# Summing softmax-free attention denominators without TensorE: seven of eight units by copies between partition groups

## The chip, the cores and the metric

The kernel runs on one core of a Trainium2 chip. The core has a matrix engine (TensorE, PE in the profile), a vector engine (VectorE, DVE), an engine for pointwise functions (ScalarE, ACT), a general engine (GpSimd, POOL) and one that issues transfers (SyncE, SP). On-chip memory (SBUF) has 128 partitions, and so has PSUM, in which TensorE puts its results, in banks of 512 fp32 columns. The metric is the device time of one execution, in microseconds (us).

## The reference

Two independent blocks of linear attention, A and B, whose outputs are put side by side. S is 2048 tokens, D is 640, and there are 32 heads of 20.

```python
qkv = (x @ wqkv).reshape(B, S, 3, H, Dh)            # q, k, v by head
phi = lambda t: where(t > 0, t + 1, exp(t)) + 1e-6
pq, pk = phi(q), phi(k)
kv  = einsum("bhsd,bhse->bhde", pk, v)
z   = einsum("bhsd->bhd", pk)
num = einsum("bhqd,bhde->bhqe", pq, kv)
den = einsum("bhqd,bhd->bhq", pq, z)[..., None] + 1e-6
out = (num / den) @ wo
```

The denominator is one number for each token and head: the sum of that head's 20 features of pq, each weighted by z.

## The kernel before

Matrices are multiplied in a 32-bit form of reduced precision. A factor is split into a high part, rounded by a ScalarE copy, and a low part, the difference, made by VectorE; a product is the sum of three matmuls, high by high, high by low and low by high. The first half of the kernel works on keys and values under a planner and is untouched. It ends at about 290 us. For each block it leaves z, and a matrix M (values and the output weights folded together), so that the output of a token is its pq, divided by its denominators, times M.

The second half goes over eight units of 512 tokens, four of block A (0 to 3) and four of block B (4 to 7). Its order is written out by hand: the loop at the end of the function calls, for each unit u, five query steps and then the output of unit u - 1. A query step (`qmm`, lines 924 to 926) is 15 matmuls of 512 columns for one of five groups of 128 features, followed by `qphi`, exp and relu on ScalarE (L1092, L1093) and their join on VectorE (L1094), and `qacc`, which adds the features weighted by z into an accumulator of 128 partitions by 512 tokens (L1102 on ScalarE for the first group, L1104 on VectorE for the others).

Features lie so that partition p holds head p mod 32. So after five groups the accumulator holds four partial sums for each head, in partitions 0 to 31, 32 to 63, 64 to 95 and 96 to 127. To add these four and have the sum in all four places at once, the kernel multiplies by the constant matrix `same`, which has a 1 where two partitions agree mod 32. This is the chain of the denominators: `split_acc` (high part on ScalarE at L918, low part on VectorE at L915), `denmm` (two matmuls into PSUM, L1114 and L1115), `recip` (a reciprocal on VectorE for each half of 256 tokens, L1120) and `divide` (L1126), which scales all of pq. Then `d_sums` (L1142 to L1147), `a_split` and `d_split` prepare the stationary factors of the output product, called da and ds, with h for high and l for low parts.

The output (`outmm`, L1203) is one level of a seven-product recursion for two 256-token halves q: 14 steps of six or nine matmuls of 320 columns. Its partial sums are the PSUM tiles pa, pe and psb. ScalarE copies pa into the output tile o (L1218), VectorE adds psb and pe (L1219). A later step goes on accumulating in the same pa, so it waits for the copy of the step before.

What stands between these is hung into slots: ("q", u, c, k) lies behind the three matmuls k of query step c of unit u, and ("o", u, s) behind output step s of unit u. The table `chain` gives the slots of the denominators' chain. Unit 0's chain runs during the queries of unit 1, that of unit v from 1 to 6 during the output of unit v - 1, and what it leaves is used in the output of v. `split` only issues ScalarE's copy; the VectorE part is kept in a list and issued at the next slot. Each engine does its own instructions in order.

Other work hangs in the same slots: the roundings of the raw queries (L962, tile xqh), of wo (tile woh, low part wol), copies of M out of PSUM (L1008, tile mev) and the forms of M for the recursion (tile fsh).

Of the kernel before, what the change touches and what calls it, by code (L numbers as in the profile page):

```python
# [7 lines left out]
F32 = mybir.dt.float32  # L8
# [3 lines left out]
AF = mybir.ActivationFunctionType  # L12
OP = mybir.AluOpType
# [205 lines left out]
def tile_linear_attn_pair(ctx: ExitStack, tc: tile.TileContext, ins, out: bass.AP):  # L219
    nc = tc.nc  # L220
    P = 128
# [19 lines left out]
    kx, kg, q1a, q1b, q2, q3 = [], [], [], [], [], []  # L241
# [435 lines left out]
    a, z, x = jh[0][0:P], jl[0][0:P], jr[0][0:P]  # L677
# [117 lines left out]
    for p in range(4, NPB):  # L795
        i, h = divmod(p - 2, 2)
# [9 lines left out]
    for p in range(NPB + 1, NP):  # L806
        if p == NPB + 1:
            fl = kvs
        else:
            i, h = divmod(p - NPB - 2, 2)  # L810
# [70 lines left out]
    for g, (h0, nh) in enumerate(GROUPS):  # L881
        cols = NC * DH * nh
        w = Space("wv", cols, (BD,))
# [17 lines left out]
    def bank(name, tag="one", bufs=3):  # L901
        at, n = ptags[tag]
        pn[tag] = pn.get(tag, -1) + 1
        return psum.tile([P, 512], F32, name=name, tag=f"bank{at + pn[tag] % n}", bufs=1)
# [165 lines left out]
    pq, acc, den, dd = {}, {}, {}, {}  # L1070
# [39 lines left out]

    def denmm(u):
        t = acc.pop(u)
        ps = den.pop(u) if u in den else bank("psd", "small", 1)
        nc.tensor.matmul(ps, same, t[:, 0], start=True, stop=False)  # L1114
        nc.tensor.matmul(ps, same, t[:, 1], start=False, stop=True)  # L1115
        den[u] = (ps, q2[0].tile([P, 512], F32, name="rd", tag="rd", bufs=1))

    def recip(u, h):
        ps, r = den[u]
        nc.vector.reciprocal(r[:, h * 256:(h + 1) * 256], ps[:, h * 256:(h + 1) * 256])  # L1120

    def divide(u, h):

        r = den[u][1][:, h * 256:(h + 1) * 256].unsqueeze(1).to_broadcast([P, NC, 256])
        p = pq[u][:, :, h * 256:(h + 1) * 256]
        nc.vector.scalar_tensor_tensor(p, p, EPS, r, op0=OP.add, op1=OP.mult)  # L1126

    da, ds, sr = {}, {}, {}
# [161 lines left out]
    h = NG - 1  # L1290
# [8 lines left out]
    for c in range(NC):  # L1299
# [3 lines left out]
        for u in range(1, NU - 1):  # L1303
# [3 lines left out]

    at(("q", 1, 0, 0), z_end)

    den[0] = bank("psd", "small", 1)  # L1310

    chain = {
        0: [(("q", 1, 0, 0), split_acc, 0), (("q", 1, 1, 1), denmm, 0), (("q", 1, 1, 1), recip, 0, 0),
            (("q", 1, 1, 1), recip, 0, 1), (("q", 1, 1, 2), divide, 0, 0), (("q", 1, 1, 4), divide, 0, 1),
            (("q", 1, 2, 0), d_sums, 0, 0), (("q", 1, 2, 2), a_split, 0, 0), (("q", 1, 2, 4), d_sums, 0, 1),
            (("q", 1, 3, 1), d_split, 0, 0), (("q", 1, 3, 4), a_split, 0, 1), (("q", 1, 4, 1), d_split, 0, 1)]}
    for v in range(1, NU):
        w, u = v - 1, v + 1
        if v == NU - 1:
            chain[v] = [(("o", w, 1), split_acc, v), (("o", w, 4), denmm, v), (("o", w, 4), recip, v, 0),  # L1320
                        (("o", w, 5), divide, v, 0), (("o", w, 6), a_split, v, 0, 0), (("o", w, 6), d_sums, v, 0, 0),
                        (("o", w, 7), d_split, v, 0, 0), (("o", w, 8), a_split, v, 1, 0), (("o", w, 8), d_sums, v, 1, 0),
                        (("o", w, 9), recip, v, 1), (("o", w, 10), d_split, v, 1, 0), (("o", w, 12), divide, v, 1),
                        (("o", v, 0), a_split, v, 0, 1), (("o", w, 13), d_sums, v, 0, 1),
                        (("o", v, 0), d_split, v, 0, 1), (("o", v, 2), d_sums, v, 1, 1),
                        (("o", v, 2), a_split, v, 1, 1), (("o", v, 3), d_split, v, 1, 1)]
        elif v == 1:
            chain[v] = [(("o", w, 4), split_acc, v), (("o", w, 7), denmm, v), (("o", w, 8), recip, v, 0),
                        (("o", w, 10), recip, v, 1), (("o", w, 11), divide, v, 0),
                         (("o", w, 12), divide, v, 1), (("q", u, 0, 2), d_sums, v, 0), (("q", u, 0, 4), a_split, v, 0),  # L1330
                         (("q", u, 1, 2), d_sums, v, 1), (("q", u, 2, 1), d_split, v, 0), (("q", u, 3, 1), a_split, v, 1),
                         (("q", u, 3, 4), d_split, v, 1)]
        else:
            chain[v] = [(("o", w, 2), split_acc, v), (("o", w, 5), denmm, v), (("o", w, 7), recip, v, 0),
                        (("o", w, 9), recip, v, 1), (("o", w, 11), divide, v, 0),
                         (("o", w, 12), divide, v, 1), (("q", u, 0, 2), d_sums, v, 0), (("q", u, 0, 4), a_split, v, 0),
                         (("q", u, 1, 2), d_sums, v, 1), (("q", u, 2, 1), d_split, v, 0), (("q", u, 3, 1), a_split, v, 1),
                         (("q", u, 3, 4), d_split, v, 1)]
    for v in range(NU):
        for a, f, *x in chain[v]:  # L1340
            at(a, f, *x)
# [63 lines left out]
```

## Time and profile before

| | |
|---|---|
| median of 3 runs | 570.86 us (570.66 to 571.42) |
| the profiled execution | 570.49 us, of which the profile's span is 568.7 |
| PE, matmuls | 564.2 us busy, 99% of the span |
| DVE | 434.2 us, 76% |
| ACT | 341.4 us, 60% |
| POOL | 62.9 us, 11% |
| granted TensorE clock | 1.0 of full speed |

Busy times of different engines lie beside each other. A matmul's row gives its start and a modelled duration, and the next one starts before it has ended. In rows of groups the first number after the bar is the busy time of the group, the second the mean duration of one instruction in ns. In rows of a timeline the first number is the start in us from the begin of the span, the second the duration of the row.

### The profile page before, as it was taken

The page shows a single profiled execution, that of the slowest core. Times are in us where ns is not written, and L with a number is a line of the kernel's source. Part 1 is how long each engine was busy: PE and PEld are TensorE (multiplying, and loading weights), DVE is VectorE, ACT ScalarE, POOL GpSimd, SP SyncE. Part 2 cuts the span into 40 slices and gives each one's busy share as a digit, 9 for nine tenths or more (in the row PEclk, how much of TensorE's full clock was granted, in tenths as well). Part 3 has the DMA queues.
Part 4 walks back from the last instruction along what each step waited for, and adds up shares of the span by engine and source line. Part 5 has one row for each costly group of instructions (what it writes and reads, how often), then busy time and mean ns, then how long its engine had stood idle before and what let it go on. Part 6 is the DMA issues. An engine that isn't in the chain of part 4 may idle for free.

```text
span 568.7 us, 9488 instructions
## 1 busy us (share of the span) xinstructions
PE 564.2 (99%) x3524; PEld 536.0 (94%) x3524; DVE 434.2 (76%) x706; ACT 341.4 (60%) x619; POOL 62.9 (11%) x103
## 2 busy tenths in 40 slices
PE   9999999999999999999999999999999999999997
PEld 7999999999999999999988899898989989898997
DVE  6888687598888767888645899977788776758792
ACT  6878566673788756766436665646656464644551
POOL 0210011110001021110010103110011201001010
PEclk9999999999999999999999999999999999999999
DMA  8993755758849676697999967662454996122022
GB/s 294 370 283 118 198 150 125 238 142 248 262 116 274 180 190 181 199 295 202 352 281 342 355 238 258 228 193 95 146 202 144 366 391 224 42 76 93 0 93 92
DMA packets 68321, 117.64 MB, mean 207 GB/s; under 512 B 6804, under 2 KB 30132, under 8 KB 68276
## 3 DMA queue, kind: packets, MB, share of 16 engines
q1 hardware_dynamic: 59060, 89.94, 48.0%
q0 software_dynamic: 8928, 26.92, 17.0%
q8 instruction: 27, 0.44, 0.3%
q10 hardware_dynamic: 288, 0.20, 0.1%
q14 instruction: 18, 0.15, 0.1%
HBM read 71.13 MB, written 35.41 MB: 187 GB/s over the span
## 4 chain that ended last, share of the span: by engine, by line
PE 99%; DVE 0%; issue 0%
PE psg L316 25%; PE pa L1203 12%; PE ka L316 10%; PE psq L924 8%; PE psq L926 8%; PE psq L925 8%; PE pe L1203 6%; PE ke L316 5%; PE psk L719 4%; PE psb L1203 4%; PE kb L316 3%; PE pskv L556 1%; PE pskv L984 1%; PE psm L583 1%; PE psi L647 1%; PE psk L696 1%
## 5 line engine op out<-in xcount | busy, mean ns | idle before, releaser
L316 PE MATMUL psg<-pkl,xnh 128*128 128x320 f32 x320 | 98.9, 309 | 0.0
L316 PE MATMUL psg<-pkh,xnh 128*128 128x320 f32 x320 | 98.8, 309 | 0.0
L316 PE MATMUL psg<-pkh,xnl 128*128 128x320 f32 x320 | 98.5, 308 | 0.0
L924 PE MATMUL psq<-xqh,wh 128*128 128x512 f32 x200 | 78.5, 393 | 0.0
L926 PE MATMUL psq<-xqh,wl 128*128 128x512 f32 x200 | 78.0, 390 | 0.0
L925 PE MATMUL psq<-xql,wh 128*128 128x512 f32 x200 | 77.9, 390 | 0.0
L316 PEld LDWEIGHTS psg<-pkl,xnh 128*128 128x128 f32 x320 | 60.1, 188 | 0.0
L316 PEld LDWEIGHTS psg<-pkh,xnl 128*128 128x128 f32 x320 | 60.1, 188 | 0.0
L316 PEld LDWEIGHTS psg<-pkh,xnh 128*128 128x128 f32 x320 | 60.0, 188 | 0.0
L489 ACT ACTIVATE kt<-ka 128x320 f32<-128x320 f32 x52 | 22.7, 437 | 59.1 <-PE ka L316 59.0
L1218 ACT ACTIVATE o<-pa 128x320 f32<-128x320 f32 x64 | 27.9, 438 | 45.2 <-PE pa L1203 45.0
L406 POOL DMA_DIRECT2D zacc<-ek x32 | 26.6, 840 | 236.1 <-DVE ek L499 173.7
L1094 DVE SCALAR_TENSOR_TENSOR pq<-eq,rq 128x512 f32<-128x512 f32 x40 | 27.7, 691 | 30.7 <-ACT rq L1093 30.6
L537 DVE TENSOR_TENSOR gacc<-psg,gacc 128x320 f32<-128x320 f32 x60 | 29.4, 489 | 23.5 <-PE psg L316 22.5
L1092 ACT ACTIVATE eq<-psq 128x512 f32<-128x512 f32 x40 | 23.9, 597 | 36.9 <-PE psq L926 34.8
L926 PEld LDWEIGHTS psq<-xqh,wl 128*128 128x128 f32 x200 | 37.5, 188 | 7.9
L925 PEld LDWEIGHTS psq<-xql,wh 128*128 128x128 f32 x200 | 37.6, 188 | 7.6 <-DMA xql<-xd 0.2
L924 PEld LDWEIGHTS psq<-xqh,wh 128*128 128x128 f32 x200 | 37.6, 188 | 7.1
L401 ACT ACTIVATE pkh<-ek,epst 128x640 fp32r<-128x640 f32 x32 | 26.5, 828 | 6.9 <-DVE ek L499 6.7
L1203 PE MATMUL pa<-fh,dal 128*128 128x320 f32 x96 | 29.7, 309 | 0.0
L1203 PE MATMUL pa<-fh,dah 128*128 128x320 f32 x96 | 29.7, 309 | 0.0
L1203 PE MATMUL pa<-fl,dah 128*128 128x320 f32 x96 | 29.7, 309 | 0.0
(215 smaller groups left out, 1558.2 us busy)
## 6 DMA issues: line engine op xcount, KB each, us to landing
zacc<-ek POOLq DMA_DIRECT2D x32, 320.0 KB, 4.8
xql<-xd SPq DMA_DIRECT2D x40, 256.0 KB, 5.0
xd<-xl SPq DMA_DIRECT2D x29, 320.0 KB, 3.9
out<-o POOLq DMA_DIRECT2D x28, 320.0 KB, 3.6
xns<-in_A_x SPq DMA_DIRECT2D x16, 320.0 KB, 5.4
xts<-in_B_xt_tiles SPq DMA_DIRECT2D x16, 320.0 KB, 3.6
xns<-in_B_x SPq DMA_DIRECT2D x16, 320.0 KB, 5.8
xqs<-in_A_xt SPq DMA_DIRECT2D x20, 256.0 KB, 5.8
```

Source lines behind the costliest of these rows:

```text
L316: nc.tensor.matmul(o, a.r, w.r, start=start and k == i == 0, stop=k == n - 1 and i == 2, skip_group_check=True)
L401: note("ACT", n + 110, lambda: act(hi.r, p.f, AF.Identity, bias=epst), [hi], [p, K0.all], by=8.0)
L406: note("POOL", 1.0, lambda: nc.gpsimd.dma_start(z.f, p.f, **kw), [z], [p], dma=1.0 if first else 1.86)
L537: tt(o, BK[k].tile[:, :HF], o, op=OP.add)
L719: nc.tensor.matmul(o[h][:, :HF], x[a].r, w[c][h * HF:h * HF + HF].r, start=c == 0 and i == 0, stop=c == NC - 1 and i == 2, skip_group_chec ...
L924: nc.tensor.matmul(o, whi, xhi, start=first, stop=False)
L925: nc.tensor.matmul(o, whi, xlo, start=False, stop=False)
L926: nc.tensor.matmul(o, wlo, xhi, start=False, stop=last)
L1092: nc.scalar.activation(e, ps, AF.Exp)
L1094: nc.vector.scalar_tensor_tensor(pq[u][:, c, :], e, 1.0, r, op0=OP.min, op1=OP.add)
L1203: nc.tensor.matmul(ps, x, y, start=start and n == i == 0, stop=n == len(terms) - 1 and i == 2, skip_group_check=True)
L1218: copy = lambda x, y: nc.scalar.activation(x, y, AF.Copy)
```

## The change

For units 0 to 6 the multiplication by `same` is replaced by adding the partition groups themselves. `fold1` copies on ScalarE the upper 64 partitions of the accumulator's first 256 tokens to the lower 64, and the lower 64 of the other 256 tokens to the upper 64. `fold2` adds on VectorE, so that partitions 0 to 63 hold the first 256 tokens and 64 to 127 the others, two partial sums each. `fold3` exchanges by four ScalarE copies the 32-partition groups within each half, `fold4` adds and takes one reciprocal of 128 by 256, which covers all 512 tokens, and `fold5` spreads it by four ScalarE copies to the tile rd, 128 by 512, that `divide` reads. The low part of the accumulator isn't needed any more. Unit 7 keeps the matmuls. The slots of the chain change with it: unit 0's divisions stand two slots or so later, unit 1's chain begins one output step earlier.

```diff
+    def fold1(u):
+        t = q2[0].tile([P, 2, 512], F32, name="ac", tag="sr", bufs=2)
+        a = acc[u]
+        nc.scalar.activation(t[0:64, 0, 0:256], a[64:128, 0:256], AF.Copy)
+        nc.scalar.activation(t[64:128, 0, 0:256], a[0:64, 256:512], AF.Copy)
+        den[u] = t
+
+    def fold2(u):
+        t, a = den[u], acc.pop(u)
+        for p, c in ((0, 0), (64, 256)):
+            rows = slice(p, p + 64)
+            nc.vector.tensor_tensor(t[rows, 0, 256:512], a[rows, c:c + 256], t[rows, 0, 0:256], op=OP.add)
+
+    def fold3(u, h):
+        t = den[u]
+        for p, q in ((0, 32), (32, 0)):
+            p, q = p + 64 * h, q + 64 * h
+            nc.scalar.activation(t[p:p + 32, 1, 0:256], t[q:q + 32, 0, 256:512], AF.Copy)
+
+    def fold4(u):
+        t = den[u]
+        nc.vector.tensor_tensor(t[:, 1, 0:256], t[:, 0, 256:512], t[:, 1, 0:256], op=OP.add)
+        nc.vector.reciprocal(t[:, 1, 256:512], t[:, 1, 0:256])
+        den[u] = (t, q2[0].tile([P, 512], F32, name="rd", tag="rd", bufs=1))
+
+    def fold5(u, h):
+        t, r = den[u]
+        for p in (0, 64):
+            nc.scalar.activation(r[p:p + 64, h * 256:(h + 1) * 256], t[64 * h:64 * h + 64, 1, 256:512], AF.Copy)
...
-        0: [(("q", 1, 0, 0), split_acc, 0), (("q", 1, 1, 1), denmm, 0), (("q", 1, 1, 1), recip, 0, 0),
-            (("q", 1, 1, 1), recip, 0, 1), (("q", 1, 1, 2), divide, 0, 0), (("q", 1, 1, 4), divide, 0, 1),
+        0: [(("q", 1, 0, 0), fold1, 0), (("q", 1, 0, 2), fold2, 0), (("q", 1, 0, 3), fold3, 0, 0),
+            (("q", 1, 0, 4), fold3, 0, 1), (("q", 1, 1, 1), fold4, 0), (("q", 1, 1, 3), fold5, 0, 0),
+            (("q", 1, 1, 4), fold5, 0, 1), (("q", 1, 1, 4), divide, 0, 0), (("q", 1, 2, 0), divide, 0, 1),
...
+            a = (3, 4, 5, 6, 7, 9, 10) if v == 1 else (2, 3, 4, 5, 6, 8, 9)
+            chain[v] = [(("o", w, a[0]), fold1, v), (("o", w, a[1]), fold2, v), (("o", w, a[2]), fold3, v, 0),
+                        (("o", w, a[3]), fold3, v, 1), (("o", w, a[4]), fold4, v), (("o", w, a[5]), fold5, v, 0),
+                        (("o", w, a[6]), fold5, v, 1), (("o", w, 11), divide, v, 0), (("o", w, 12), divide, v, 1),
```

ScalarE before, from the rounding of unit 0's accumulator (L918 ac) during unit 1's queries on:

```order
L918 ACTIVATE ac<-acc 128x512
L918 ACTIVATE woh<-wo 80x640 x2
L1092 ACTIVATE eq<-psq 128x512
L1093 ACTIVATE rq<-psq 128x512
L1102 ACTIVATE acc<-pq,zs,z 128x512
L1008 ACTIVATE mev<-psm 80x320 x2
L1092 ACTIVATE eq<-psq 128x512
```

and the same place now, where L1126 and L1127 are `fold1`, L1140 is `fold3` and L1151 is `fold5`:

```order
L1126 ACTIVATE ac<-acc 64x256
L1127 ACTIVATE ac<-acc 64x256
L918 ACTIVATE woh<-wo 80x640 x2
L1140 ACTIVATE ac<-ac 32x256 x4
L1092 ACTIVATE eq<-psq 128x512
L1093 ACTIVATE rq<-psq 128x512
L1102 ACTIVATE acc<-pq,zs,z 128x512
L1008 ACTIVATE mev<-psm 80x320 x2
L1151 ACTIVATE rd<-ac 64x256 x4
L1092 ACTIVATE eq<-psq 128x512
```

Four copies now stand ahead of the exp and relu of unit 1's first feature group, and four ahead of those of the second.

VectorE at the same place, unit 0's chain between the feature groups of unit 1 (L1134 is `fold2`, L1144 and L1145 are `fold4`, L1157 and L1173 the lines that were L1126 and L1142):

```order
-L915 TENSOR_TENSOR ac<-acc,ac 128x512
-L915 TENSOR_TENSOR wol<-wo,woh 80x640 x2
-L1094 SCALAR_TENSOR_TENSOR pq<-eq,rq 128x512
-L1120 RECIPROCAL rd<-psd 128x256 x2
...
+L915 TENSOR_TENSOR wol<-wo,woh 80x640
+L1134 TENSOR_TENSOR ac<-acc,ac 64x256 x2
+L915 TENSOR_TENSOR wol<-wo,woh 80x640
+L1094 SCALAR_TENSOR_TENSOR pq<-eq,rq 128x512
+L1144 TENSOR_TENSOR ac<-ac 128x256
+L1145 RECIPROCAL ac<-ac 128x256
+L1157 SCALAR_TENSOR_TENSOR pq<-pq,rd 128x5x256
+L1094 SCALAR_TENSOR_TENSOR pq<-eq,rq 128x512
+L1104 SCALAR_TENSOR_TENSOR acc<-pq,z,acc 128x512
+L1157 SCALAR_TENSOR_TENSOR pq<-pq,rd 128x5x256
```

The additions stand behind a subtraction for wo, and the second division stands behind the second feature group's join and accumulation instead of ahead of them.

ScalarE during the output of unit 0 (L1249 is the copy out of PSUM that was L1218), now:

```order
L1249 ACTIVATE o<-pa 128x320 x2
L1126 ACTIVATE ac<-acc 64x256
L1127 ACTIVATE ac<-acc 64x256
L1249 ACTIVATE o<-pa 128x320
L962 ACTIVATE xqh<-xqs 128x512
L1249 ACTIVATE o<-pa 128x320
L1140 ACTIVATE ac<-ac 32x256 x2
L962 ACTIVATE xqh<-xqs 128x512
L1140 ACTIVATE ac<-ac 32x256 x2
L918 ACTIVATE fsh<-wst 128x640
L1249 ACTIVATE o<-pa 128x320
```

Before, the first unit 1 instruction here was the one rounding of its accumulator, and it stood behind a third copy out of PSUM.

## Rows read from the trace of the kernel before

**Rows 1.** The page, chain that ended last: shares of the span by engine.
```profile
PE 99%; DVE 0%; issue 0%
```

**Rows 2.** Timeline of PE, query matmuls: start us, us, engine, line, op, out<-in.
```profile
308.06 0.39 PE L924 MATMUL psq<-xqh,wh 128*128 128x512 f32 x1
...
311.23 0.39 PE L926 MATMUL psq<-xqh,wl 128*128 128x512 f32 x1
```

**Rows 3.** Stretches: length, then busy us of PE, PEld, DVE, ACT, POOL; clock, DMA.
```profile
318.00:335.00 17.00, 17.00 (x86) 14.47 (x85) 16.82 (x20) 11.45 (x21) 1.18 (x2) 1.00 0.92 331
...
401.00:418.00 17.00, 17.00 (x111) 16.54 (x111) 14.57 (x19) 10.16 (x20) 1.67 (x4) 1.00 0.68 227
```

**Rows 4.** Timeline of PE around unit 0's denominator matmuls.
```profile
318.10 0.40 PE L1114 MATMUL psd<-ac,same 128*128 128x512 f32 x1
...
318.64 0.39 PE L924 MATMUL psq<-xqh,wh 128*128 128x512 f32 x1
```

**Rows 5.** Groups by line and shape, DVE, 286 us to the end: busy us, mean ns.
```profile
L1120 DVE RECIPROCAL rd<-psd 128x256 f32<-128x256 f32 x16 | 27.9, 1746 | 0.9 <-PE psd L1115 0.9
...
L1126 DVE SCALAR_TENSOR_TENSOR pq<-pq,rd 128x1280 f32<-128x1280 f32 x16 | 23.3, 1463 | 0.0
...
L1142 DVE TENSOR_TENSOR sr<-pq 128x256 f32<-128x256 f32 x2 | 0.8, 416 | 0.0
```

**Rows 6.** Groups by line and shape, ACT, 286 us to the end.
```profile
L918 ACT ACTIVATE ac<-acc 128x512 fp32r<-128x512 f32 x8 | 5.0, 631 | 5.3 <-DVE acc L1104 5.3
...
L918 ACT ACTIVATE wh<-wst 128x640 fp32r<-128x640 f32 x5 | 3.7, 732 | 0.2 <-DMA wst<-in_B_wq 0.2
...
L918 ACT ACTIVATE dah<-pq 128x256 fp32r<-128x256 f32 x7 | 2.9, 416 | 0.0
...
L918 ACT ACTIVATE woh<-wo 80x640 fp32r<-80x640 f32 x2 | 1.3, 722 | 0.0
```

**Rows 7.** Timeline of ACT, unit 0's chain in unit 1's queries.
```profile
316.89 0.63 ACT L918 ACTIVATE ac<-acc 128x512 fp32r<-128x512 f32 x1 [1.55 <-DVE acc L1104]
317.43 1.35 ACT L918 ACTIVATE woh<-wo 80x640 fp32r<-80x640 f32 x2
318.69 0.58 ACT L1092 ACTIVATE eq<-psq 128x512 f32<-128x512 f32 x1
319.16 0.58 ACT L1093 ACTIVATE rq<-psq 128x512 f32<-128x512 f32 x1
```

**Rows 8.** Timeline of DVE, the same stretch and on into unit 0's output.
```profile
316.11 0.75 DVE L1104 SCALAR_TENSOR_TENSOR acc<-pq,z,acc 128x512 f32<-128x512 f32 x1
...
318.19 1.55 DVE L915 TENSOR_TENSOR wol<-wo,woh 80x640 fp32r<-80x640 f32 x2
319.77 0.69 DVE L1094 SCALAR_TENSOR_TENSOR pq<-eq,rq 128x512 f32<-128x512 f32 x1
320.38 3.36 DVE L1120 RECIPROCAL rd<-psd 128x256 f32<-128x256 f32 x2
...
327.80 0.68 DVE L1142 TENSOR_TENSOR sr<-pq 128x512 f32<-128x512 f32 x1
...
332.85 1.22 DVE L915 TENSOR_TENSOR dsl<-sr,dsh 128x1024 fp32r<-128x1024 f32 x1
...
338.44 0.75 DVE L1104 SCALAR_TENSOR_TENSOR acc<-pq,z,acc 128x512 f32<-128x512 f32 x1
```

**Rows 9.** Timeline of PE, unit 0's output.
```profile
334.76 0.31 PE L1203 MATMUL pe<-fh,dsl 128*128 128x320 f32 x1
...
336.24 0.42 PE L1203 MATMUL pa<-fh,dsh 128*128 128x320 f32 x1
...
343.84 0.31 PE L1203 MATMUL pa<-fh,dah 128*128 128x320 f32 x1
```

**Rows 10.** Timeline of ACT, copies out of PSUM in unit 0's output.
```profile
335.74 0.78 ACT L1218 ACTIVATE o<-pa 128x320 f32<-128x320 f32 x2
...
342.72 0.44 ACT L1218 ACTIVATE o<-pa 128x320 f32<-128x320 f32 x1 [0.43 <-PE pa L1203]
```

More of the change, by code (lines that the diff above doesn't have):

```diff
@@ L1112, in denmm @@
         t = acc.pop(u)
-        ps = den.pop(u) if u in den else bank("psd", "small", 1)
+        ps = bank("psd", "small", 1)
         nc.tensor.matmul(ps, same, t[:, 0], start=True, stop=False)
@@ L1308, in tile_linear_attn_pair @@
     at(("q", 1, 0, 0), z_end)
-    den[0] = bank("psd", "small", 1)
     chain = {
-        0: [(("q", 1, 0, 0), split_acc, 0), (("q", 1, 1, 1), denmm, 0), (("q", 1, 1, 1), recip, 0, 0),
-            (("q", 1, 1, 1), recip, 0, 1), (("q", 1, 1, 2), divide, 0, 0), (("q", 1, 1, 4), divide, 0, 1),
+        0: [(("q", 1, 0, 0), fold1, 0), (("q", 1, 0, 2), fold2, 0), (("q", 1, 0, 3), fold3, 0, 0),
+            (("q", 1, 0, 4), fold3, 0, 1), (("q", 1, 1, 1), fold4, 0), (("q", 1, 1, 3), fold5, 0, 0),
+            (("q", 1, 1, 4), fold5, 0, 1), (("q", 1, 1, 4), divide, 0, 0), (("q", 1, 2, 0), divide, 0, 1),
             (("q", 1, 2, 0), d_sums, 0, 0), (("q", 1, 2, 2), a_split, 0, 0), (("q", 1, 2, 4), d_sums, 0, 1),
@@ L1326, in tile_linear_attn_pair @@
                         (("o", v, 2), a_split, v, 1, 1), (("o", v, 3), d_split, v, 1, 1)]
[L1327 to L1332, printed above, removed]
-        else:
[L1334 to L1338, printed above, removed]
+        else:
+            a = (3, 4, 5, 6, 7, 9, 10) if v == 1 else (2, 3, 4, 5, 6, 8, 9)
+            chain[v] = [(("o", w, a[0]), fold1, v), (("o", w, a[1]), fold2, v), (("o", w, a[2]), fold3, v, 0),
+                        (("o", w, a[3]), fold3, v, 1), (("o", w, a[4]), fold4, v), (("o", w, a[5]), fold5, v, 0),
+                        (("o", w, a[6]), fold5, v, 1), (("o", w, 11), divide, v, 0), (("o", w, 12), divide, v, 1),
+                        (("q", u, 0, 2), d_sums, v, 0), (("q", u, 0, 4), a_split, v, 0), (("q", u, 1, 2), d_sums, v, 1),
+                        (("q", u, 2, 1), d_split, v, 0), (("q", u, 3, 1), a_split, v, 1),
+                        (("q", u, 3, 4), d_split, v, 1)]
     for v in range(NU):
```

## Prediction

> **What bounds the kernel now.** I read the page's chain first: what ended last is TensorE for 99% of the span, with 0% for VectorE and for issue [rows 1]. So the time is TensorE's instruction stream: a change wins by shortening that stream and loses by making TensorE stand. A matmul's listed duration is not its price, since matmuls overlap; its price is the distance between starts. TensorE's timeline in an undisturbed stretch gives it: from 308.06 to 311.23 us lie 14 steps between 512-column matmuls, 3.17 us, 0.226 each [rows 2]. Last I read, by stretches, how much room the helping engines have. While TensorE multiplies unit 1's queries (318 to 335 us), VectorE is busy 16.82 of 17.00 us and ScalarE 11.45; in a later unit's stretch (401 to 418) they are 14.57 and 10.16 [rows 3]. VectorE is full just where unit 0's denominators are made, so a delay there isn't made good before unit 0's output matmuls.
>
> **What is removed.** Seven units lose both denominator matmuls: 14 x 0.226 = 3.17 us. Around unit 0's pair the starts go from 318.10 to 318.64, so that pair cost 0.54, some 0.09 more than two steps [rows 4]. Together 3.26 us: 0.54 in unit 0 and 6 x 0.452 = 2.71 in units 1 to 6. On VectorE each of these units loses one of two reciprocals of 1.746 us and a subtraction [rows 5]; on ScalarE the rounding copy, 0.631 and once for each of the eight units [rows 6].
>
> **What is added.** Ten ScalarE copies of 256 columns a unit, two VectorE additions on 64 partitions and one on 128. The nearest row for such a copy is the 128x256 one from SBUF to SBUF: 0.416 us [rows 6]. That fewer partitions would make it shorter the rows don't say: 640 columns take 0.722 on 80 partitions and 0.732 on 128 [rows 6]. Successive copies on ScalarE start before the one before has ended: from 317.43 to 318.69 pass two of 0.722, so they start 0.63 apart [rows 6, 7]. So the price of a copy is 0.31 if it overlaps its neighbour likewise, and 0.416 + 0.03 = 0.45 if it has to wait for its end (0.03 lies between the end of VectorE's accumulation, 316.11 + 0.75, and the copy that it releases at 316.89 [rows 7, 8]). No row shows a copy from one group of partitions to another. I take 0.31, the row nearest in size and memory, and keep 0.45 as the dear end; the cheap end is half the data for half the partitions, 0.21. The additions of 256 columns I take at 0.42 [rows 5], 0.34 apart, since a VectorE instruction of 0.69 is followed after 0.61 [rows 8]. The reciprocal now reads SBUF instead of PSUM; I leave it at 1.75.
>
> **Unit 0, step by step.** Here the chain stands on the path. Times are in the clock of the profiled run.
> - The first two copies start when the accumulator is ready, at 316.89 like the rounding copy before [rows 7]. At 0.31 each they bring the first wo rounding to 317.51, its end to 318.23; a second wo rounding behind it leaves ScalarE free at 318.77.
> - VectorE now has the first wo subtraction, which waits for that rounding, ahead of the additions: 318.26, and 0.74 later (two take 1.55 [rows 8]) the additions, 319.00 and 319.34, the first ending at 319.42.
> - ScalarE's four 32-partition copies stand ahead of unit 1's exp and relu. They wait until 319.45 and take 1.24, so exp starts at 320.69 instead of 318.69; relu starts 0.47 later and lasts 0.58 [rows 7]. VectorE's first product of unit 1 starts at 321.77 instead of 319.77 [rows 8]: 2.00 late.
> - From there to the first sums of unit 0's left side it was 327.80 - 319.77 = 8.03 us, VectorE always busy [rows 8]. Now: 0.61 to the addition, 0.45 to the reciprocal, 1.75; at 2.81 two copies are needed before the first division (0.03 + 0.31 + 0.42 + 0.03 = 0.79), which is issued at 3.60 and takes 1.46 [rows 5]; unit 1's next product waits for an exp and a relu behind four copies (2.84 + 1.24 + 0.47 + 0.58 + 0.03) and starts at 5.16; the accumulation 0.72 later, the second division another 0.67 on, and 1.46 + 0.03 to the sums: 8.04. What the missing reciprocal and subtraction save is eaten by the waits for copies.
> - So the sums come 2.01 late, and VectorE, full as it is, keeps that up to the low part of those sums: it started at 332.85 and lasted 1.22, and ends now at 336.08 [rows 8].
> - TensorE used it at 334.76 [rows 9] and would be there 0.54 earlier. It gets it at 336.11: 1.35 behind its old schedule instead of 0.54 ahead, 1.89 us of standing.
> - The copies of the first output partial sums out of PSUM stand behind unit 1's last exp and relu, which wait for that same VectorE queue: 335.74 [rows 10] becomes 337.75, with its own 0.45 (two take 0.78) and the release 338.23. TensorE wants the first of them at 336.24 + 1.35 = 337.59 [rows 9]: 0.64 more. It is 1.99 behind.
> - Unit 1's first copies wait for its accumulator, 338.44 + 0.75 [rows 8] + 2.01 + 0.03 = 341.23, and now stand ahead of a copy out of PSUM. From there ScalarE has a queue without gaps (six fold copies, two copies out of PSUM, two roundings of x, one of a form: 1.86 + 0.66 + 1.04 + 0.63 = 4.19) up to the copy that stood at 342.72 [rows 10]: 345.42, released 345.89. The matmul that needs it, at 343.84 [rows 9], would come at 345.83: 0.06.
>
> Unit 0 leaves TensorE 2.05 us behind, though two of its matmuls are gone.
>
> **The other units.** There the chain runs inside the previous unit's output matmuls, and its result is wanted a whole unit later. ScalarE gains 10 x 0.31 - 0.53 = 2.6 us on some 10.2 of 17, VectorE loses over a microsecond [rows 3]. The nearest wait is the copy out of PSUM between two output steps of nine matmuls; a rounding of x and two fold copies, 1.14 in all, fit into such a step of 1.33 us (ten matmul steps from 334.76 to 336.24, 0.148 each [rows 9]). I cost these units at nothing, so 2.71 us are kept.
>
> **Sum.** -2.71 + 2.05 = -0.66 us. The profiled execution took 570.49 us (span 568.7 and 1.8 around it), 0.37 under the median of 570.86; I apply the difference to the median: 570.2 us.
>
> **Rivals.**
> - *Copies that change the partition group don't overlap (slower).* Each then costs 0.45, and so does the step to the one behind. In unit 0 the first two copies add 0.28, the next four 0.56, the last four 0.56 by way of exp and relu: the sums come 3.4 late instead of 2.0. TensorE gets the low part 2.75 behind its old schedule; the copy out of PSUM adds 0.64, ScalarE's queue is 0.84 longer and ends in another 0.9: 4.3 behind. Against 2.71 kept that is +1.6; with a tenth or two from units where the copy out of PSUM is then late, +1.8: 572.7 us. Slower than before begins at a spacing of about 0.36. For it: the ten copies go between groups and alternate, and the overlap in the rows is shown for equal groups only. Against it: ScalarE's roundings overlap on 80 partitions as on 128.
>   The Trainium skill (VectorE: DVE Perf Modes, section "Two Vector instructions with no wait between them") says that a Vector instruction whose input or output starts in another group of 32 partitions than that of the instruction before is held until the earlier ones have finished. It speaks of VectorE only, and no row here shows a case. By it the second addition would start 0.11 later, which nothing on the path waits for; if ScalarE does the same, this rival's time follows.
> - *Copies are cheap on few partitions (faster).* At 0.21 apart unit 1's product is 1.4 late and the sums 1.1; TensorE is 0.45 behind, 0.6 more by the copy out of PSUM, nothing after it: -2.71 + 1.05, 569.2 us. The 80-partition row speaks against it.
> - *No standing at all* (unit 0's chain has room that I don't see): the whole 3.26, 567.6 us. Against it: VectorE's 16.82 of 17.00.
>
> **Chances.** Forecast 0.46, its own range 569.4 to 571.2; no overlap 0.37, 571.8 to 573.4; cheap copies 0.14; no standing 0.03. About 0.2%, 1.1 us, is what a measurement of this kernel can tell from no change. Faster by more: the last two and the lower edge of the forecast, 0.21. Slower: nearly all of the second, 0.36. The same: 0.43. Range 569.0 to 573.0: it leaves out the lower half of the cheap cases and the edge of the dear one.
>
> **What the new profile would show.** I am right if TensorE stands about 1.9 us by the first output steps of unit 0 (near 335 us), released by VectorE's low part, then about 0.6 released by a ScalarE copy, and hardly anywhere later, with fold copies 0.41 long and 0.31 apart. Copies 0.42 to 0.45 apart and about 1 us of standing after 344 show the slower rival; a first stand under 1 us shows the cheap copies. The sum, not a size in it, is wrong if TensorE stands in units 2 to 6.

## The result and the profile after

The changed kernel takes 573.36 us (median of 6 runs, 573.03 to 574.16), the kernel before, on the same chip, 571.09 (6 runs). The ratio is 1.0043, interval 1.003 to 1.0056: slower, by 2.3 us. The forecast was 570.2 with a range of 569.0 to 573.0; what came is the rival *copies that change the partition group don't overlap* (572.7, own range 571.8 to 573.4).

The profiled execution has a span of 571.7 us against 568.7. Its first query matmuls already start 0.35 later, which the change can't have caused: the copies begin only at 317 us. So I read spans from one place in the program, which I call the mark: of the query matmuls near 290 us one is listed at 0.47 us, the only one of its line there. It starts between 289.7 and 290.9 us in the profiles of this study, and from its start to the end of the span it is 278.9 us before and 281.6 after, 2.7 more. (The row here is the one of before; that of after is the first row of TensorE's timeline below.)

```profile
289.76 0.47 PE L924 MATMUL psq<-xqh,wh 128*128 128x512 f32 x1
```

The page's chain of the changed kernel. Where TensorE had 99% [rows 1], the shares no longer add up to the span, so I read it only for names: ScalarE's fold copy L1140 and its copy out of PSUM L1249 have joined the chain.

```profile
PE 38%; ACT 0%; issue 0%; DVE 0%
PE pa L1234 11%; PE psq L926 6%; PE psq L925 6%; PE psq L924 6%; PE pe L1234 6%; PE psb L1234 3%; ACT fsh L918 0%; DVE o L1250 0%; ACT ac L1140 0%; ACT o L1249 0%; PE psd L1114 0%; PE psd L1115 0%
```

The first of the two stretches of [rows 3], after (us; busy PE, PEld, DVE, ACT, POOL; clock, DMA share, GB/s):

```profile
318.00:335.00 17.00, 15.93 (x77) 13.06 (x76) 12.95 (x16) 12.53 (x25) 1.18 (x2) 1.00 0.87 306
```

VectorE was busy 16.82 us in it and now is 12.95. It gets through 16 instructions there where it had 20, and stands in between; PE has lost a microsecond. The clock is granted in full, as before.

**Why VectorE stands: ScalarE's timeline**, the place of [rows 7]:

```profile
317.25 0.42 ACT L1126 ACTIVATE ac<-acc 64x256 f32<-64x256 f32 x1 [1.55 <-DVE acc L1104]
317.68 0.42 ACT L1127 ACTIVATE ac<-acc 64x256 f32<-64x256 f32 x1
318.11 1.37 ACT L918 ACTIVATE woh<-wo 80x640 fp32r<-80x640 f32 x2
320.06 1.70 ACT L1140 ACTIVATE ac<-ac 32x256 f32<-32x256 f32 x4 [0.59 <-DVE ac L1134]
321.78 0.60 ACT L1092 ACTIVATE eq<-psq 128x512 f32<-128x512 f32 x1
322.28 0.59 ACT L1093 ACTIVATE rq<-psq 128x512 f32<-128x512 f32 x1
```

The copy's duration is as estimated, 0.42. The distance is not: 0.43 from one to the next (317.25, 317.68, 318.11), and four in 1.70 us, while exp and relu, which stay in one group, still start 0.50 apart at 0.60 long. The same holds all through the second half. I take the ScalarE instructions that start before, or within 0.1 us after, the end of the one in front, and read from the code in which group of 32 partitions each starts. In 92 of them the output's group differs from that of the one in front, or the SBUF input's from that of the last one that read SBUF. All 92 start after that end, by 0.011 to 0.026 us. Of the 155 others 150 start before it, by 0.105 in the median (the other five, 0.001 to 0.086 after it, read what TensorE has put into PSUM). In 38 of the 92 only the output's group changes, in 19 only the input's, in 35 both.

VectorE at the place of [rows 8]:

```profile
318.88 0.82 DVE L915 TENSOR_TENSOR wol<-wo,woh 80x640 fp32r<-80x640 f32 x1 [0.97 <-ACT woh L918]
319.62 0.86 DVE L1134 TENSOR_TENSOR ac<-acc,ac 64x256 f32<-64x256 f32 x2
...
322.90 0.69 DVE L1094 SCALAR_TENSOR_TENSOR pq<-eq,rq 128x512 f32<-128x512 f32 x1 [1.57 <-ACT rq L1093]
323.51 0.42 DVE L1144 TENSOR_TENSOR ac<-ac 128x256 f32<-128x256 f32 x1
323.96 1.75 DVE L1145 RECIPROCAL ac<-ac 128x256 f32<-128x256 f32 x1
326.63 1.49 DVE L1157 SCALAR_TENSOR_TENSOR pq<-pq,rd 128x1280 f32<-128x1280 f32 x1 [0.91 <-ACT rd L1151]
328.61 0.69 DVE L1094 SCALAR_TENSOR_TENSOR pq<-eq,rq 128x512 f32<-128x512 f32 x1 [0.49 <-ACT rq L1093]
...
336.59 1.22 DVE L915 TENSOR_TENSOR dsl<-sr,dsh 128x1024 fp32r<-128x1024 f32 x1
```

The idle times in brackets are nearly the whole story of VectorE: 0.97, 1.57, 0.91 and 0.49 us, each ended by ScalarE. Unit 1's first product starts at 322.90 against 319.77, 2.78 late once the 0.35 is taken off; the low part of the left side's sums, 336.59 against 332.85, is 3.39 late.

**What TensorE waits for.** Its timeline, with the start of the queries first and then the places where it stands (335.86 to 340 answers to [rows 9]):

```profile
290.11 0.47 PE L924 MATMUL psq<-xqh,wh 128*128 128x512 f32 x1
...
319.04 0.31 PE L924 MATMUL psm<-woh,kvh 80*80 80x320 f32 x1
319.75 0.37 PE L925 MATMUL psm<-wol,kvh 80*80 80x320 f32 x1 [0.40 <-DVE wol L915]
...
333.16 0.30 PE L1234 MATMUL pa<-fl,dah 128*128 128x320 f32 x1
334.14 0.41 PE L1234 MATMUL pa<-fh,dal 128*128 128x320 f32 x1 [0.67 <-DVE dal L915]
...
335.86 0.31 PE L1234 MATMUL pe<-fl,dsh 128*128 128x320 f32 x1
337.87 0.41 PE L1234 MATMUL pe<-fh,dsl 128*128 128x320 f32 x1 [1.70 <-DVE dsl L915]
338.12 0.31 PE L1234 MATMUL pe<-fh,dsh 128*128 128x320 f32 x1
...
339.29 0.31 PE L1234 MATMUL pe<-fh,dsl 128*128 128x320 f32 x1
339.98 0.41 PE L1234 MATMUL pa<-fh,dsh 128*128 128x320 f32 x1 [0.37 <-ACT o L1249]
...
346.97 0.31 PE L1234 MATMUL pa<-fh,dal 128*128 128x320 f32 x1
348.65 0.41 PE L1234 MATMUL pa<-fh,dah 128*128 128x320 f32 x1 [1.37 <-ACT o L1249]
...
415.68 0.31 PE L1234 MATMUL pa<-fh,dal 128*128 128x320 f32 x1
415.96 0.42 PE L1234 MATMUL pa<-fh,dah 128*128 128x320 f32 x1
416.21 0.31 PE L1234 MATMUL pa<-fl,dah 128*128 128x320 f32 x1
```

A 320-column step is 0.147. What exceeds it between two starts is standing ("stand" below): 0.57, 0.83, 1.86 and 0.54 in unit 0, 1.53 in unit 1 (346.97 to 348.65), 0.13 in unit 3 (415.68 to 415.96) and 0.12 likewise in unit 4. Behind each stand the next step is long too, 0.25 instead of 0.147 (337.87 to 338.12); that is about 0.10 a stand, 0.07 behind the first. Together 4.18 us in unit 0, 1.64 in unit 1, 0.47 in units 3 and 4: 6.3 in all. Against it stand 3.26 of matmuls removed and the 0.10 that the step from 336.24 took too long before [rows 9]: +2.9 us, where the stretch from the mark shows +2.7 and the medians +2.3. The remaining 0.2 is spread over steps of a few hundredths that I didn't trace. The rows of before around that step:

```profile
336.08 0.31 PE L1203 MATMUL pe<-fh,dsl 128*128 128x320 f32 x1
...
336.49 0.31 PE L1203 MATMUL pa<-fl,dsh 128*128 128x320 f32 x1
```

### The profile page after: what moved, and what is told of

Read it like the earlier page. It is cut to its first block, busy times and chain, and to the rows that moved or that the text cites. A ratio compares the mean times of both kernels' runs of the same rounds, so it can differ in the third digit from the quotient of the medians.

```text
span 571.7 us, 9528 instructions
## 1 busy us (share of the span) xinstructions
PE 562.4 (98%) x3510; PEld 533.0 (93%) x3510; DVE 428.1 (75%) x713; ACT 366.6 (64%) x682; POOL 62.9 (11%) x103
## 5 line engine op out<-in xcount | busy, mean ns | idle before, releaser
L1249 ACT ACTIVATE o<-pa 128x320 f32<-128x320 f32 x64 | 27.8, 436 | 22.6 <-PE pa L1234 22.0
```

The costliest lines, as they stand in the source:

```text
L1249: copy = lambda x, y: nc.scalar.activation(x, y, AF.Copy)
```

## The experiments

Each is timed against the kernel before on the same chip: the changed kernel against the 571.09 us above, the next four against 570.81 (27 runs), the last three, on another chip, against 570.88 (14 runs). "From the mark" is the stretch defined above, of one profile each (before 278.9).

| kernel | median us (runs) | ratio, interval | from the mark |
|---|---|---|---|
| changed kernel | 573.36 (6) | 1.0043, 1.003 to 1.0056 | 281.6 |
| unit 0 by matmuls, 1 to 6 by copies | 570.16 (11) | 0.9989, 0.998 to 0.9998 | 278.2 |
| only unit 0 by copies | 573.97 (5) | 1.0053, 1.0041 to 1.0066 | 282.3 |
| copies within one group | 570.72 (11) | 0.9996, 0.9987 to 1.0005 | 278.9 |
| last four copies one way | 571.01 (11) | 1.0006, 0.9997 to 1.0015 | 279.1 |
| units 2 to 6 by copies | 569.37 (10) | 0.9975, 0.9966 to 0.9984 | 277.1 |
| units 1 to 6, unit 1 later | 568.75 (5) | 0.9961, 0.9947 to 0.9974 | 276.6 |
| and units 3 and 4 later | 568.69 (5) | 0.9958, 0.9946 to 0.9971 | 276.1 |

**Which units cost.** First unit 0 gets its old chain back, its steps too:

```diff
-        0: [(("q", 1, 0, 0), fold1, 0), (("q", 1, 0, 2), fold2, 0), (("q", 1, 0, 3), fold3, 0, 0),
...
+        0: [(("q", 1, 0, 0), split_acc, 0), (("q", 1, 1, 1), denmm, 0), (("q", 1, 1, 1), recip, 0, 0),
+            (("q", 1, 1, 1), recip, 0, 1), (("q", 1, 1, 2), divide, 0, 0), (("q", 1, 1, 4), divide, 0, 1),
...
```

> Unit 0 keeps the two matmuls and its old slots; units 1 to 6 are summed by copies as in the changed kernel. Theory (the loss sits in unit 0's chain, and the standing near 347 us belongs to unit 1's own copies in unit 0's output): TensorE still stands about 1.4 us near the copy out of PSUM in unit 0's output and hardly elsewhere, so 12 x 0.226 = 2.71 saved less about 1.4: 1.2 to 1.5 us under the kernel before. Rival (the standing near 347 is only unit 0's lateness handed on): it goes too, 2.5 to 2.9 us under the kernel before. If units 1 to 6 cost more than unit 0, the time stays over that of the kernel before.

And the reverse, only unit 0 by copies:

```diff
-            a = (3, 4, 5, 6, 7, 9, 10) if v == 1 else (2, 3, 4, 5, 6, 8, 9)
-            chain[v] = [(("o", w, a[0]), fold1, v), (("o", w, a[1]), fold2, v), (("o", w, a[2]), fold3, v, 0),
...
+            chain[v] = [(("o", w, 2), split_acc, v), (("o", w, 5), denmm, v), (("o", w, 7), recip, v, 0),
+                        (("o", w, 9), recip, v, 1), (("o", w, 11), divide, v, 0),
...
```

> Only unit 0 is summed by copies; units 1 to 7 keep their matmuls and old slots. Theory: 0.54 us of matmuls go and TensorE stands 3.6 to 3.8 us (0.5 near 319, 0.8 and 1.9 at the first output steps, 0.5 at the first copy out of PSUM), so 3.0 to 3.3 us over the kernel before, more than the whole change costs. Rival (the loss is spread over the units): under 1 us over the kernel before.

Measured: 0.65 us under before for the first and 3.16 over for the second. So unit 0's loss is the changed kernel's whole loss, and more. Alone it shows unit 0's stands to the hundredth (0.57, 0.83, 1.86, 0.54) and none near 347. The other six units gain less than their matmuls: without unit 0 by copies, unit 1 makes the same 1.53, so it isn't unit 0's lateness that causes it. TensorE there:

```profile
343.64 0.31 PE L1234 MATMUL pa<-fh,dal 128*128 128x320 f32 x1
345.32 0.41 PE L1234 MATMUL pa<-fh,dah 128*128 128x320 f32 x1 [1.37 <-ACT o L1249]
```

and ScalarE, which releases it:

```profile
339.63 0.42 ACT L1126 ACTIVATE ac<-acc 64x256 f32<-64x256 f32 x1 [2.71 <-DVE acc L1104]
340.07 0.42 ACT L1127 ACTIVATE ac<-acc 64x256 f32<-64x256 f32 x1
340.51 0.44 ACT L1249 ACTIVATE o<-pa 128x320 f32<-128x320 f32 x1
...
344.85 0.42 ACT L1249 ACTIVATE o<-pa 128x320 f32<-128x320 f32 x1
```

ScalarE is idle for 2.71 us in front of unit 1's first copy, with copies out of PSUM queued behind it, and then has no gap until 345.27. In microseconds of TensorE the six units give 12 x 0.2275 = 2.73 less 1.53, 0.13 and 0.12 and 0.10 behind each: 0.65, the measured number. (One thing is not as before: the PSUM bank of unit 0's two matmuls is no longer reserved ahead of the queries. That pair takes 0.63 us of TensorE here and 0.54 before; why isn't shown.) I had expected 1.2 to 1.5; what was left out was the time behind each stand, the stands of units 3 and 4 and part of unit 1's.

**Group change or copy.** The next kernel has as many copies of 256 columns at the same steps, some on more partitions than the changed kernel's, but all of them start at partition 0 on both sides. It leaves out the exchange between the groups, and so the sums.

```diff
-            nc.scalar.activation(r[p:p + 64, h * 256:(h + 1) * 256], t[64 * h:64 * h + 64, 1, 256:512], AF.Copy)
...
+        for o in (t[0:64, h, 0:256], r[:, h * 256:(h + 1) * 256]):
+            nc.scalar.activation(o, t[0:o.shape[0], 1, 256:512], AF.Copy)
```

> As many copies of 256 columns at the same places for units 0 to 6, but every copy reads and writes from partition 0 on (32, 64 or 128 partitions); groups are not exchanged, so the denominators are not summed over the four groups. Theory (ScalarE waits for the end of the instruction before whenever the 32-partition group in which it starts to read or write changes): copies start 0.31 apart as other ScalarE work does, and the time is the one of the forecast, 0.3 to 0.7 us under the kernel before. Rival (copies of 32 and 64 partitions, or copies that don't round, never overlap): the copies of 32 and 64 partitions stay 0.43 apart, and the time stays 1.5 to 2.3 us over the kernel before.

Measured 0.1 us under before (interval 0.7 under to 0.3 over), less than the 0.3 to 0.7 expected, and 2.4 under the changed kernel when each is compared with its own runs of before. ScalarE's last four copies of unit 0 in its trace:

```profile
325.71 0.42 ACT L1151 ACTIVATE ac<-ac 64x256 f32<-64x256 f32 x1 [0.72 <-DVE ac L1146]
326.04 0.40 ACT L1151 ACTIVATE rd<-ac 128x256 f32<-128x256 f32 x1
326.34 0.40 ACT L1151 ACTIVATE ac<-ac 64x256 f32<-64x256 f32 x1
326.65 0.40 ACT L1151 ACTIVATE rd<-ac 128x256 f32<-128x256 f32 x1
```

0.31 apart, on 64 partitions as on 128: the spacing that I had forecast. TensorE's stands shrink to 0.32, 1.80 and 0.54 in unit 0 and 0.47 in unit 1, and those of units 3 and 4 are gone. The one of unit 1:

```profile
346.40 0.31 PE L1234 MATMUL pa<-fh,dal 128*128 128x320 f32 x1
347.01 0.42 PE L1234 MATMUL pa<-fh,dah 128*128 128x320 f32 x1 [0.30 <-ACT o L1249]
```

With the long step behind each, the stands add up to 3.5 us where the changed kernel has 6.3; the two stretches from the mark differ by the same 2.8. That is the price of the group changes, with the waits that follow from them. The other 3.5 stay without them, most of it in unit 0 (2.95 of its 4.18), and use up the 3.3 that the removed matmuls give: even with copies that overlap, this placement would only break even.

Is it the way across that costs, or the change from one instruction to the next? In the last variant of this kind the four final copies all read from partition 64 and write from partition 0; the others start at partition 0 on both sides, as in the kernel just told of, though some write to other tiles or on more partitions.

```diff
+        for o in (t[0:64, h, 0:256], r[0:64, h * 256:(h + 1) * 256]):
+            nc.scalar.activation(o, t[64:128, 1, 256:512], AF.Copy)
```

> Like the run with equal groups, but the four copies behind the reciprocal all read from partition 64 on and write from partition 0 on, so each crosses groups and none changes the group against the one before it; the denominators are again not the right sums. Theory (the change of group holds ScalarE, not the crossing): within these four the spacing is 0.31, only the first of them and the next instruction that reads on-chip memory from partition 0 start 0.01 after an end; 0.1 to 0.5 us under the kernel before. Rival (a copy that crosses groups or starts off partition 0 doesn't overlap): these four are 0.43 apart, and the time is 0.2 to 0.8 us over the kernel before.

```profile
510.82 0.42 ACT L1150 ACTIVATE ac<-ac 64x256 f32<-64x256 f32 x1
511.14 0.40 ACT L1150 ACTIVATE rd<-ac 64x256 f32<-64x256 f32 x1
511.44 0.41 ACT L1248 ACTIVATE o<-pa 128x320 f32<-128x320 f32 x1
511.76 0.40 ACT L1150 ACTIVATE ac<-ac 64x256 f32<-64x256 f32 x1
512.07 0.40 ACT L1150 ACTIVATE rd<-ac 64x256 f32<-64x256 f32 x1
```

In unit 6 here: two copies that both cross follow each other at 0.32 and 0.31. So a copy that crosses is not dear in itself; the change against its predecessor is. Nor does the copy out of PSUM between them wait or make wait: its input lies in another memory, its output in the same group. The same spacings stand in all seven units. The time is 0.2 us over before (interval 0.2 under to 0.9 over), not the 0.1 to 0.5 under that I expected, and at the lower end of what the rival had; medians can't tell this kernel from the one just told of, so it is the spacing that decides between the two.

**Where the remaining loss of units 1 to 6 sits.** In the next kernel units 0 and 1 use matmuls; the edit gives unit 1 the old chain of steps, as unit 0 has in the first experiment.

```diff
+        elif v == 1:
+            chain[v] = [(("o", w, 4), split_acc, v), (("o", w, 7), denmm, v), (("o", w, 8), recip, v, 0),
...
```

> Units 0 and 1 keep their 14 and 14 TensorE matmuls' worth of denominators as before (two matmuls each), at their old steps; units 2 to 6 sum by copies. Theory (the copies of units 0 and 1 fall where another engine's work is due at once, those of units 2 to 6 do not): ten matmuls of 0.2275 us go, 2.28 us, less the 0.13 and 0.12 us that TensorE stood in units 3 and 4 and about 0.10 us behind each, so 1.8 us under before, ratio 0.9968; no stand near 344. Rival (a stand moves on to the next unit that sums by copies: unit 2 now stands as unit 1 did, 1.5 us and 0.10 behind it): 0.2 us under before, ratio 0.9997, with a stand of about 1.5 us near 376.

The other keeps unit 1's copies and moves them behind two more copies out of PSUM:

```diff
-            a = (3, 4, 5, 6, 7, 9, 10) if v == 1 else (2, 3, 4, 5, 6, 8, 9)
+            a = (5, 5, 6, 8, 8, 10, 10) if v == 1 else (2, 3, 4, 5, 6, 8, 9)
```

> Unit 0 by matmuls and units 1 to 6 by copies as in the first experiment, but unit 1's seven pieces of the sum start later: at steps 5, 5, 6, 8, 8, 10, 10 of the unit's output chunks in place of 3, 4, 5, 6, 7, 9, 10. Theory (unit 1's first copies stood on ScalarE ahead of the copy out of PSUM that step (5,0) waits for; later, they do not): the 1.53 us and the 0.10 behind it go, twelve matmuls of 0.2275 us less 0.13, 0.12 and 0.10 behind each, about 2.3 us under before, ratio 0.996. Rival (later pieces make unit 1's divide late, and TensorE stands at the first output product of unit 1 instead): no better than the 0.65 us of the first experiment, with a stand of over 1 us between 355 and 385.

and the last moves the final copies of units 3 and 4 as well:

```diff
-            a = (5, 5, 6, 8, 8, 10, 10) if v == 1 else (2, 3, 4, 5, 6, 8, 9)
+            a = (5, 5, 6, 8, 8, 10, 10) if v == 1 else (2, 3, 4, 5, 6, 10, 10) if v in (3, 4) else (2, 3, 4, 5, 6, 8, 9)
```

> As the one with unit 1's pieces later, and units 3 and 4 run their last two pieces at steps 10 and 10 in place of 8 and 9. Theory: the stands of 0.13 and 0.12 us near 412 and 445 and the 0.10 behind each go too, 2.7 us under before, ratio 0.9952. Rival: the divide of those units comes late and stands cost as much or more than they did; 2.3 us under before or worse.

Measured 1.5, 2.1 and 2.2 us under before by the medians, 1.9, 2.3 and 2.8 by the stretch from the mark; expected were 1.8, 2.3 and 2.7. With unit 1 moved, ScalarE has taken two more copies out of PSUM before it waits:

```profile
337.92 0.44 ACT L1249 ACTIVATE o<-pa 128x320 f32<-128x320 f32 x1 [0.91 <-PE pa L1234]
338.25 0.62 ACT L962 ACTIVATE xqh<-xqs 128x512 fp32r<-128x512 f32 x1
338.80 0.44 ACT L1249 ACTIVATE o<-pa 128x320 f32<-128x320 f32 x1
339.71 0.42 ACT L1126 ACTIVATE ac<-acc 64x256 f32<-64x256 f32 x1 [0.48 <-DVE acc L1104]
```

and TensorE passes the place of the 1.53 without standing:

```profile
343.73 0.31 PE L1234 MATMUL pa<-fh,dal 128*128 128x320 f32 x1
343.88 0.31 PE L1234 MATMUL pa<-fh,dah 128*128 128x320 f32 x1
```

In the last kernel the two small stands are gone from the profile too; the medians don't separate it from the one before it. It has the lowest median here: 568.69 us, 0.42% under before, where the change as made is 0.43% over.

## Why the prediction was wrong

The step that failed is the one between two ends: the fold copy at "0.31 if it overlaps its neighbour likewise", against 0.45. I took the row nearest in size and memory; what decides is not size but whether the group changes, and no row of before had a change. 0.43 was measured, and with the change taken away 0.31 at once. By the prediction's own count slower than before begins at about 0.36. Three smaller terms were too low as well, and the experiment with copies in one group shows them without the hold: unit 1's stand (0.47 where I had 0.06), the wait for wo's low part (0.32 where I had none) and the long step behind each stand (0.07 to 0.10, which I hadn't counted). I use "hold" for a start that waits for the end of the instruction in front because the group changes.

Point by point:

- *What bounds the kernel*: right. Every loss found is a stand of TensorE, and the two matmuls a unit are worth their steps.
- *Copy 0.42 long, additions 0.42, reciprocal 1.75 from SBUF*: right. The two 64-partition additions on VectorE, of which the second works in another group, take 0.86 together, 0.44 apart instead of the 0.34 I used; nothing waited for it.
- *Unit 0, first product 2.00 late*: 2.78. The rival's sum, with 0.28 and 0.56 for six held copies, gives 2.84.
- *Low part of the sums 2.01 late*: 3.39; the rival had 3.4.
- *1.89 of standing near 335*: 3.54 in all, with what follows each stand, but in three places, since the subtraction for wo and the low part of the first half come late as well (0.57 at 319, 0.83 at 333). I named only the last of these waits, which sets how late TensorE is in the end; the earlier ones take a part of it.
- *0.64 at the first copy out of PSUM*: 0.54 and 0.10 behind it.
- *0.06 near 346*: 1.53 and 0.11. I had ScalarE's queue there right in its parts, 4.19 us from unit 1's first copy to the copy out of PSUM that TensorE needs; it took 5.22 (342.97 to 348.19 after). The difference, 1.03, is eight held starts of about 0.13 (0.10 of overlap lost and 0.01 to 0.03 of distance): five copies and three instructions that follow a copy in another group. With copies in one group the same queue takes 4.16, as summed, and the stand is 0.47, so 1.06 of the 1.53 is the hold.
- *The other units at nothing*: failed at a smaller scale, 0.13 and 0.12 in units 3 and 4, and 0.11 behind each; the prediction named standing in units 2 to 6 as what would make its sum wrong. With copies in one group both are gone, with the last two pieces a step or two later also.
- *The sum, −0.66 us*: the kernel that has the spacing I assumed measures −0.1 (interval −0.7 to +0.3). The interval reaches down to my sum; by the one profile, 0.1 under before in the stretch from the mark, even at 0.31 my sum was about half a microsecond too low, mainly by the three smaller terms named above.
- *Chances*: 0.37 for the rival that came true, with its end at 573.4, yet the range ended at 573.0. The mechanism of that rival was right, and its size nearly: +1.8 us against the +2.3 measured. Not all its terms were: it had 0.9 for unit 1's stand, which with the step behind it is 1.64, and a tenth or two for units 2 to 6, where 0.47 came.

The Trainium skill (VectorE: DVE Perf Modes, section "Two Vector instructions with no wait between them") gives this hold for VectorE: an instruction whose input or output starts in another group of 32 partitions than the last one in the same memory waits for the earlier ones to finish. The pair of additions in unit 0 agrees, 0.44 apart at 0.41 long. The section speaks of VectorE; the runs here show the same on ScalarE, in 92 of 92 successions, and the copy out of PSUM between crossing copies fits its "same memory" too. The Trainium skill (ScalarE: Activation LUTs, section "What ACT_TABLE_LOAD costs") has back-to-back ScalarE instructions overlap by about 0.093 us; the traces agree where the groups stay, about 0.10, and not where one changes. I had read the VectorE section as a reason for the rival and gave it too little weight: the open question was only whether a second engine behaves alike.

What stays open: why the weight load in front of a long step isn't done ahead (see the last section), and whether ScalarE's hold also applies to a change of group inside PSUM, which no ScalarE instruction of the second half makes.

## What to carry to other kernels

Matmuls removed from a full TensorE are a gain only where the work that replaces them has room in time, so look for where its result is wanted at once (the first unit of a pipeline) and leave the matmuls there. Copies between partition groups should be priced at their full duration on both sides, or ordered so that successive instructions start in the same groups; and an instruction that waits for a late accumulator belongs behind the copies out of PSUM that are due meanwhile, not ahead of them.

## What the hardware showed unexpectedly

- A ScalarE instruction that waits for nothing else starts 0.01 to 0.03 us after the end of the one in front when the start group of its output or SBUF input changes (92 of 92 in the changed kernel), and otherwise about 0.10 before that end. A 64x256 copy thus costs 0.43 instead of 0.31.
- After TensorE has stood, the first matmul is listed at 0.41 us instead of 0.31 and the second comes 0.25 behind it instead of 0.147: each stand costs 0.10 more than itself, 0.102 to 0.108 in all fifteen stands of the output matmuls in four profiles (the changed kernel, unit 0 alone, units 1 to 6 alone, copies within one group). The long step isn't tied to the length of the stand: before, the step from 336.24 to 336.49 is 0.25 long, and the one in front of it, from 336.08, only 0.16.

What goes with the long step is the weight load (PEld), the loading of the matmul's stationary factor. In an undisturbed row it starts about 0.14 us ahead of its matmul; behind a stand it starts together with it (the matmuls of these two loads start at 335.86 and 337.87):

```profile
335.71 0.19 PEld L1234 LDWEIGHTS pe<-fl,dsh 128*128 128x128 f32 x1
337.87 0.19 PEld L1234 LDWEIGHTS pe<-fh,dsl 128*128 128x128 f32 x1 [1.96 <-DVE dsl L915]
```

Of the 900 matmuls of 320 columns that the changed kernel has behind the mark, seven have a load that starts within 0.002 us of them, those behind its seven stands; the loads of the other 893 start 0.137 us or more ahead. Before, the one at 336.24 is the only one of 900. At 348.65 the profile names a copy out of PSUM as what TensorE waited for, not a factor, and still the load wasn't done ahead.
